# Rounding float64 weights on the chip: products on GpSimd, ScalarE's results in PSUM, two units' scores made earlier

## The chip, the cores and the metric

The kernel runs on one core of a Trainium2 chip. The metric is the device time of one execution in microseconds (us); the median of nine executions of the kernel before is 1681.1 us.

## The reference

Eight batches of eight heads attend over 576 tokens with 64 channels per head. Of each row of scores only the 32 largest are kept. The result, as 4608 tokens of 512 channels, goes through two matrix products with a leaky ReLU between them.

```python
scores = scale * np.matmul(q, k.transpose(0, 1, 3, 2))      # (8, 8, 576, 576)
kth = np.partition(scores, -32, axis=-1)[..., -32:-31]
scores = np.where(scores >= kth, scores, -1000000000.0)
attn = softmax(scores)                                       # with 1e-9 added to the sum
x = (attn @ v).transpose(0, 2, 1, 3).reshape(4608, 512)
h = x @ w_in                                                 # (4608, 2048)
out = np.maximum(0.01 * h, h) @ w_out                        # (4608, 512)
```

`w_in` (512 x 2048) and `w_out` (2048 x 512) arrive as float64. The host passes their bits as pairs of 32-bit words, and the kernel makes float32 of them itself.

## The kernel before, in words

**Units.** Attention is cut into 144 units. A unit is 128 rows of scores for both heads of a pair. It passes through these steps, on the engines named: `scores` (TensorE into the PSUM tiles `psc0` and `psc1`, then two ScalarE copies into `s_sb`), `top_k` on VectorE (eight MAX8 and six MATCH_REPLACE8 over 576 columns, lines 195 and 198), `mask` on GpSimd (for each head a TENSOR_SCALAR, line 209, and a TENSOR_TENSOR, line 211), `exponents` and `normalize` on ScalarE, transposes on TensorE with ScalarE copies, `weigh_values` on TensorE, and a ScalarE copy into `x` (line 272).

**Steps.** The instruction order on each engine is written out by hand. The loop over `s` takes in each step one unit through `top_k`, the one before through `mask`, the one before that through `exponents`, and so on, and it issues `scores` for the unit two steps ahead. After each 256 tokens (128 for the first two chunks) the two products of that chunk, `mlp`, become available. They are issued in portions between the other work: `ph` (line 282, `x` times `w_in`), a leaky ReLU on ScalarE into `gT` (line 288), then `pz` (line 294, `gT` times `w_out`).

**The gap.** After the first four units come six steps without a new unit (`gap`). In them the weights are converted, in 16 chunks of 128 x 1024 values: eight of `w_in`, then eight of `w_out`. Slots 1 to 3 of each gap step call `convert`, so there are 18 calls. The products of the first chunk of 128 tokens are also issued in the gap, and so are the scores of the fifth and the sixth unit (units 4 and 5, counted from 0), after slot 0 of the last two gap steps. These are the first units whose `top_k` follows the gap.

**One chunk.** A chunk's raw words lie in one of three `raw` buffers, `lo` and `hi` interleaved. On VectorE, line 110 takes the exponent field out of `hi`, line 111 the upper mantissa bits (written straight into the weight tile `dst`). Every other chunk (`on_vector`) is clamped by line 114 on VectorE and shifted by line 115 on ScalarE; the others are clamped and shifted by three ScalarE instructions, lines 117 to 119. ScalarE's line 120 turns the low word into `frac`, in place in `raw`. Two calls later three VectorE instructions finish the chunk: line 122 adds the two parts of the mantissa, line 124 puts the sign into the power of two, line 126 multiplies. Lines 122, 124 and 126 each read two tiles of SBUF. Line 124 is the last reader of the raw buffer; the fetch of the chunk three later waits for it on SyncE's queue, which issues all DMAs.

Of the kernel before, what the change touches and what calls it, by code (L numbers as in the profile page):

```python
# [8 lines left out]
F32 = mybir.dt.float32  # L9
U32 = mybir.dt.uint32  # L10
AF = mybir.ActivationFunctionType
ALU = mybir.AluOpType
# [5 lines left out]
def kernel(  # L18
# [13 lines left out]
    nc = tc.nc  # L32
    NPAIR, P, S = qT.shape
# [12 lines left out]
    WCH = 1024  # L46
# [7 lines left out]
    const = ctx.enter_context(tc.tile_pool(name="const", bufs=1))  # L54
    xpool = ctx.enter_context(tc.tile_pool(name="xpool", bufs=2))
    loads = ctx.enter_context(tc.tile_pool(name="loads", bufs=LOADED))
    raws = ctx.enter_context(tc.tile_pool(name="raws", bufs=3))
    work = ctx.enter_context(tc.tile_pool(name="work", bufs=2))
    small = ctx.enter_context(tc.tile_pool(name="small", bufs=5))
    ps_sc = ctx.enter_context(tc.tile_pool(name="ps_sc", bufs=1, space=bass.MemoryType.PSUM))  # L60
# [3 lines left out]
    ident = const.tile([P, P], F32, name="ident")  # L64
    make_identity(nc, ident)

    ends = const.tile([P, 2], F32, name="ends")
    range_lo, range_hi = ends[:, 0:1], ends[:, 1:2]
    nc.vector.memset(range_lo, -896.0)
    nc.vector.memset(range_hi, 255.0)  # L70

    w_in = [const.tile([P, DFF], F32, name=f"w_in{c}") for c in range(HP)]
    w_out = [const.tile([P, 4, DMODEL], F32, name=f"w_out{c}") for c in range(NFC // 4)]
    gT = [const.tile([P, CHMAX], F32, name=f"gT{f}") for f in range(NFC)]
# [3 lines left out]
    def weight_chunks():  # L78

        words = moe_w_in.shape[1] // DFF  # L80
        for j in range(DFF // WCH):
            for c in range(HP):
                yield (w_in[c][:, j * WCH:(j + 1) * WCH],
                       moe_w_in[c * P:(c + 1) * P, j * WCH * words:(j + 1) * WCH * words])
        for f in range(0, NFC, 2):
            yield (w_out[f // 4][:, f % 4:f % 4 + 2, :],
                   moe_w_out[f * P:(f + 2) * P, :].rearrange("(g p) n -> p g n", g=2))
# [11 lines left out]
        nc.sync.dma_start(to, src)  # L99
        return dst, raw  # L100

    def convert_weights(dst, raw, on_vector):

        lo, hi = raw[:, :, 0], raw[:, :, 1]
        frac, man = lo.bitcast(F32), dst.bitcast(U32)
        ex = raws.tile([P, WCH], U32, name="ex", bufs=2)
        exf = ex.bitcast(F32)
        nc.vector.tensor_scalar(ex, hi, 20, 0x7FF, ALU.logical_shift_right, ALU.bitwise_and)  # L110
        nc.vector.tensor_scalar(man, hi, 0xFFFFF, None, ALU.bitwise_and)  # L111

        if on_vector:
            nc.vector.tensor_scalar(ex, ex, 1151.0, 896.0, ALU.min, ALU.max)  # L114
            nc.scalar.activation(ex, ex, AF.Copy, bias=-896.0 * 2.0 ** 23, scale=2.0 ** 23)
        else:
            nc.scalar.activation(exf, ex, AF.Relu, bias=range_lo, scale=1.0)
            nc.scalar.activation(exf, exf, AF.Relu, bias=range_hi, scale=-1.0)
            nc.scalar.activation(ex, exf, AF.Copy, bias=255.0 * 2.0 ** 23, scale=-2.0 ** 23)
        nc.scalar.activation(frac, lo, AF.Copy, bias=1.0, scale=2.0 ** -52)  # L120
        yield
        nc.vector.scalar_tensor_tensor(out=dst, in0=man, scalar=2.0 ** -20, in1=frac,  # L122
                                       op0=ALU.mult, op1=ALU.add)
        nc.vector.scalar_tensor_tensor(out=ex, in0=hi, scalar=0x80000000, in1=ex,  # L124
                                       op0=ALU.bitwise_and, op1=ALU.bitwise_or)
        nc.vector.tensor_tensor(dst, dst, exf, ALU.mult)  # L126

# [2 lines left out]
    def load_qk(pi):  # L132
        qt = loads.tile([P, S], F32, name="qt")
        kt = loads.tile([P, S], F32, name="kt")
        nc.sync.dma_start(qt, qT[pi])
        nc.sync.dma_start(kt, kT[pi])
        qk_of[pi] = qt, kt

    def load_v(pi):
        v_of[pi] = loads.tile([P, NKC, 2, D], F32, name="vt", bufs=LOADED_V)  # L140
        nc.sync.dma_start(v_of[pi], vk[pi])
# [19 lines left out]
    units = []  # L161
# [8 lines left out]
    def scores(u):  # L170
        ps = [ps_sc.tile([P, 2, 512], F32, name=f"psc{i}") for i in range(2)]
        for n in range(0, len(u.parts), 2):
            for half in range(2):
                for i, pi, side, r0 in u.parts[n:n + 2]:
                    qt, kt = qk_of[pi]
                    d = slice(side * D, (side + 1) * D)
                    nc.tensor.matmul(  # L177
                        ps[i][r0:r0 + u.rows, half, 0:HS],
                        qt[d, u.q0:u.q0 + u.rows],
                        kt[d, half * HS:(half + 1) * HS],  # L180
                        start=True, stop=True,
                    )
        u.both = work.tile([P, 2, S], F32, name="s_sb", bufs=5)
        u.s = [u.both[:, i, :] for i in range(2)]
        for i in range(2):
            nc.scalar.copy(u.s[i].rearrange("p (h n) -> p h n", h=2), ps[i][:, :, 0:HS])  # L186
# [26 lines left out]
    def exponents(u, i):  # L213
        nc.scalar.activation(u.s[i], u.s[i], AF.Exp, bias=u.nbias[:, i:i + 1], scale=SCALE,  # L214
                             accum_out=u.z[:, i:i + 1])

    def sums(u):
        u.ze = small.tile([P, 2], F32, name="ze")
        nc.scalar.activation(u.ze, u.z, AF.Copy, bias=1e-9, scale=1.0)  # L219
# [109 lines left out]
    LAG = 3  # L329


    FIRST, GAP = 4, 6
    steps = units[:FIRST] + [None] * GAP + units[FIRST:]
    gap = range(FIRST, FIRST + GAP)

    def unit(n):
        return steps[n] if 0 <= n < len(steps) else None
# [17 lines left out]
    def slot_budget(s):  # L355

        after = [at for at, _ in ready_at if at >= s]
        until = gap[-1] if s in gap else after[0] if after else s
        return backlog[0] / ((until + 1 - s) * SLOTS)

    SLOTS = 7
    converting, begun = [], [0]

    chunks, raw_chunks = weight_chunks(), []

    def fetch_weights():
        chunk = next(chunks, None)
        got = load_weights(*chunk) if chunk else None
        if got:
            raw_chunks.append(got)  # L370

    def convert():

        if len(converting) == 2 or not raw_chunks:
            for c in converting[:1]:
                next(converting.pop(0), None)
        if raw_chunks:
            begun[0] += 1
            converting.append(convert_weights(*raw_chunks.pop(0), on_vector=begun[0] % 2 == 1))
            next(converting[-1])  # L380
        fetch_weights()

    with tc.manual_schedule():
        last = {p: n for n, u in enumerate(steps) if u for p in u.pairs}
        for p in range(HP):
            load_qk(p)
            if p < 2:
                scores(units[p])
        for _ in range(3):
            fetch_weights()  # L390
        for p in range(HP):
            load_v(p)

        def load_more(s):

            for of, load, n, lag in ((qk_of, load_qk, LOADED, -2), (v_of, load_v, LOADED_V, LAG)):
                while len(of) < NPAIR and (len(of) < n or last[len(of) - n] + lag <= s):
                    load(len(of))

        for s in range(len(steps) + LAG):  # L400
            cur, old = unit(s), unit(s - 1)
            older, oldest, new = unit(s - 2), unit(s - LAG), unit(s + 2)
            picks = top_k(cur) if cur else iter(())
            budget = slot_budget(s)

            def slot(n):
                next(picks, None)
                if s in gap and n:
                    convert()

            slot(0)
            if new and s in gap:
                scores(new)
            if old:
                mask(old, 0)
                mask(old, 1)
            mlp_steps(budget)
            if older:
                exponents(older, 0)
            if oldest:  # L420
                transpose_main(oldest, 0)
            mlp_steps(budget)
            if older:
                exponents(older, 1)
                sums(older)
            slot(1)
            if oldest:
                transpose_main(oldest, 1)
            mlp_steps(budget)
            if oldest:  # L430
                transpose_tail(oldest)
            slot(2)
            mlp_steps(budget)
            if older:
                reciprocals(older)
            mlp_steps(budget)
            slot(3)
            if older:
                normalize(older, 0)
                normalize(older, 1)  # L440
            if oldest:
                weigh_values(oldest)
            if new and s not in gap:
                scores(new)
            mlp_steps(budget)
            mlp_steps(budget)
            attended(s)
            if s >= gap[-1]:
                load_more(s)
        mlp_steps(1e9)  # L450
# [53 lines left out]
```

## Time and profile before

| | |
|---|---|
| median of 9 runs (lowest, highest) | 1681.1 us (1680.71, 1682.39) |
| the profiled execution: its own time | 1682.27 us |
| the profiled execution: span from first to last instruction | 1680.6 us |
| mean granted TensorE clock | 0.981 |
| TensorE busy | 1555.4 us (93%) |
| VectorE busy | 1493.5 us (89%) |
| ScalarE busy | 1005.8 us (60%) |
| GpSimd busy | 1081.3 us (64%) |
| the gap on VectorE: first line 110 to first MAX8 of unit 4 | 46.18 to 138.92 us |

In the profile PE is TensorE's matmuls, PEld its weight loads, DVE is VectorE, ACT is ScalarE, POOL is GpSimd and SP is SyncE. Shares are averages over stages of different kinds: four units alone, the gap, a stretch in which VectorE is busy all the time and TensorE is not, and then a long stretch in which TensorE is. What the gap costs is read in the gap. A VectorE instruction's record begins up to 0.08 us before the one ahead has ended, so costs in a full queue are read from start to start.

### The profile page before, as it was taken

To read this page: it belongs to the slowest core of one execution; us is meant where nothing else is said; L and a number is where in the kernel's file an instruction comes from. 1 tells how busy PE (TensorE), PEld (TensorE's weight loads), DVE (VectorE), ACT (ScalarE), POOL (GpSimd) and SP (SyncE) were. 2 spreads that over 40 slices of the span, in tenths; PEclk is the share of its full clock that TensorE was granted. 3 is DMA by queue.
4 is the path that set the end of the run, shared out by engine and by line. 5 is a ranking of instruction groups with operands and counts; after the bars stand their busy time and mean duration, and the time that the engine had idled before them with its cause. 6 is when DMAs were issued, how large, how long until landed. Compare 5 with 4: busy or idle time off the path is not lost.

```text
span 1680.6 us, 25687 instructions
## 1 busy us (share of the span) xinstructions
PE 1555.4 (93%) x9360; PEld 1057.0 (63%) x9360; DVE 1493.5 (89%) x3114; ACT 1005.8 (60%) x2277; POOL 1081.3 (64%) x726
## 2 busy tenths in 40 slices
PE   3365679999999999999999999999999999999999
PEld 2252465757576757676767676767676767676765
DVE  8999999999999999999999999999999999999700
ACT  2762566666666666666656565656565656565630
POOL 5203777777777777777777777777777777777700
PEclk9977799999999999999999999999999999999999
DMA  4451001000200011000110011000100010000000
GB/s 162 136 189 43 1 29 49 19 14 15 63 26 13 1 43 43 30 1 29 49 37 1 13 33 54 17 13 20 59 24 13 1 41 16 22 1 13 1 13 13
DMA packets 22462, 57.21 MB, mean 34 GB/s; under 512 B 2368, under 2 KB 2368, under 8 KB 21312
## 3 DMA queue, kind: packets, MB, share of 16 engines
q1 hardware_dynamic: 22336, 55.58, 9.7%
q8 instruction: 73, 1.20, 0.3%
q14 instruction: 53, 0.43, 0.1%
HBM read 46.14 MB, written 9.44 MB: 33 GB/s over the span
## 4 chain that ended last, share of the span: by engine, by line
PE 84%; DVE 14%; ACT 1%; issue 0%; DMA 0%; SPq 0%; ACTq 0%
PE ph L282 29%; PE pz L294 29%; PE po L262 10%; PE psc L177 9%; PE main L234 7%; DVE tops L195 6%; DVE rest L198 5%; PE tail L240 1%; DVE ex L124 1%; DVE w_in L126 1%; DVE w_in L122 1%; DVE ex L110 0%; DVE w_in L111 0%; ACT raw L120 0%; DVE ex L114 0%
## 5 line engine op out<-in xcount | busy, mean ns | idle before, releaser
L209 POOL TENSOR_SCALAR pen<-s_sb,tops 128x576 f32<-128x576 f32 x288 | 639.3, 2220 | 385.4 <-PE ph L282 157.7
L195 DVE MAX8 tops<-rest 128x8 f32<-128x576 f32 x864 | 607.9, 745 | 0.0
L282 PE MATMUL ph<-x,w_in 128*128 128x256 f32 (+1 forms) x2432 | 560.3, 376 | 19.5 <-ACT gT L288 14.2
L294 PE MATMUL pz<-w_out,gT 128*128 128x512 f32 x1152 | 534.8, 599 | 1.4 <-ACT gT L288 1.4
L282 PEld LDWEIGHTS ph<-x,w_in 128*128 128x128 f32 x2432 | 431.3, 194 | 104.7 <-ACT x L272 29.5
L198 DVE MATCH_REPLACE8 rest<-tops,rest 128x576 f32<-128x576 f32 x576 | 423.3, 743 | 0.0
L211 POOL TENSOR_TENSOR s_sb<-s_sb,pen 128x576 f32<-128x576 f32 x288 | 407.8, 1416 | 24.0
L294 PEld LDWEIGHTS pz<-w_out,gT 128*128 128x128 f32 x1152 | 203.3, 190 | 218.4 <-issue 215.4
L226 ACT ACTIVATE s_sb<-s_sb,rz 128x576 f32<-128x576 f32 x288 | 206.9, 768 | 75.2 <-DVE rz L223 75.1
L186 ACT COPY s_sb<-psc 128x576 f32<-128x576 f32 x288 | 169.9, 642 | 104.3 <-PE psc L177 104.3
L214 ACT ACTIVATE s_sb<-s_sb,nbias 128x576 f32<-128x576 f32 x288 | 223.5, 776 | 14.7 <-POOL s_sb L211 14.7
L235 ACT COPY wT<-main 128x512 f32<-128x512 f32 x288 | 166.2, 578 | 107.7 <-PE main L234 107.6
L288 ACT ACTIVATE gT<-ph 128x256 f32<-128x256 f32 (+1 forms) x304 | 113.1, 374 | 192.4 <-PE ph L282 192.4
L234 PE MATMUL main<-ident,s_sb 128*128 128x128 f32 x1152 | 167.0, 279 | 64.9 <-ACT s_sb L226 64.4
L262 PEld LDWEIGHTS po<-wT,vt 128*64 128x64 f32 x3200 | 164.2, 141 | 93.2 <-ACT s_sb L226 47.8
L234 PEld LDWEIGHTS main<-ident,s_sb 128*128 128x128 f32 x1152 | 141.7, 144 | 120.1 <-issue 55.9
L262 PE MATMUL po<-wT,vt 128*64 128x128 f32 (+1 forms) x3200 | 198.6, 274 | 18.5 <-ACT wT L235 18.5
L198 DVE MATCH_REPLACE8 rest<-tops,s_sb 128x576 f32<-128x576 f32 x288 | 211.6, 742 | 0.0
L195 DVE MAX8 tops<-s_sb 128x8 f32<-128x576 f32 x288 | 202.0, 743 | 6.6 <-ACT s_sb L186 6.6
L177 PE MATMUL psc<-kt,qt 64*128 64x288 f32 (+1 forms) x1280 | 189.4, 441 | 6.7 <-DMA kt<-in_kT_dram 4.5
L177 PEld LDWEIGHTS psc<-kt,qt 64*128 64x128 f32 (+1 forms) x1280 | 103.5, 182 | 50.9 <-issue 22.8
L223 DVE RECIPROCAL rz<-ze 128x2 f32<-128x2 f32 x144 | 23.6, 164 | 98.3 <-ACT ze L219 98.3
(33 smaller groups left out, 490.5 us busy)
## 6 DMA issues: line engine op xcount, KB each, us to landing
vt<-in_vk_dram SPq DMA_DIRECT2D x32, 320.0 KB, 3.1
qt<-in_qT_dram SPq DMA_DIRECT2D x32, 288.0 KB, 3.0
kt<-in_kT_dram SPq DMA_DIRECT2D x32, 288.0 KB, 3.3
out_dram<-o_sb SPq DMA_DIRECT2D x36, 256.0 KB, 2.0
raw<-in_moe_w_in_dram SPq DMA_DIRECT2D x8, 1024.0 KB, 5.3
raw<-in_moe_w_out_dram SPq DMA_DIRECT2D x8, 1024.0 KB, 4.8
```

Of the source, the lines that this page charges most:

```text
L177: nc.tensor.matmul(ps[i][r0:r0 + u.rows, half, 0:HS], qt[d, u.q0:u.q0 + u.rows], kt[d, half * HS:(half + 1) * HS], start=True, stop=True,)
L186: nc.scalar.copy(u.s[i].rearrange("p (h n) -> p h n", h=2), ps[i][:, :, 0:HS])
L195: nc.vector.max(out=u.tops[:, i, r, :], in_=src[i])
L198: nc.vector.match_replace(out=rest[i], in_to_replace=u.tops[:, i, r, :], in_values=src[i], imm_value=LOWEST)
L209: nc.gpsimd.tensor_scalar(pen, u.s[i], u.tops[:, i, ROUNDS - 1, 7:8], MASKED, ALU.is_lt, ALU.mult)
L211: nc.gpsimd.tensor_tensor(u.s[i], u.s[i], pen, ALU.add)
L214: nc.scalar.activation(u.s[i], u.s[i], AF.Exp, bias=u.nbias[:, i:i + 1], scale=SCALE, accum_out=u.z[:, i:i + 1])
L226: nc.scalar.activation(u.s[i], u.s[i], AF.Copy, bias=0.0, scale=u.rz[:, i:i + 1])
L234: nc.tensor.transpose(main[:, c, :], u.s[i][:, k0:k0 + P], ident)
L262: nc.tensor.matmul(po[side * D:(side + 1) * D, o, :], vt[:, c, side, :], u.wT[:, c + side * (NKC - 1) if c + 1 < NKC else 2 * (NKC - 1), r ...
L282: nc.tensor.matmul(ph[:, 0:n], w_in[c][:, f * P:(f + 1) * P], x[c][:, 0:n], start=(c == 0), stop=(c == HP - 1),)
L294: nc.tensor.matmul(pz[0:m, 0:DMODEL], gT[f][:, r0:r0 + m], w_out[f // 4][:, f % 4, :], start=(f == 0), stop=(f == NFC - 1),)
```

## The change

All 16 chunks are now clamped on VectorE (line 114 of before becomes line 107 and is no longer in every other chunk only), and ScalarE does two instructions for each. Their results, `frac` and `power`, go into the PSUM tiles `psc0` and `psc1`, which `scores` uses outside the gap, so the two VectorE instructions that read them now read one tile of SBUF and one of PSUM each. The final product moves from VectorE (line 126) to GpSimd (line 119). `ex` gets three buffers instead of two. The constants `ends` go.

A call of `convert` now begins a chunk (three VectorE instructions), finishes the chunk of the call before (two VectorE instructions, one GpSimd), and then issues the ScalarE part of the new one. A chunk is finished one call after it was begun, not two.

Units 4 and 5 get their scores at the ends of steps 2 and 3, before the gap, and none are issued in the gap.

```diff
-    def convert_weights(dst, raw, on_vector):
+    def convert_weights(dst, raw):
         lo, hi = raw[:, :, 0], raw[:, :, 1]
-        frac, man = lo.bitcast(F32), dst.bitcast(U32)
-        ex = raws.tile([P, WCH], U32, name="ex", bufs=2)
-        exf = ex.bitcast(F32)
+        man = dst.bitcast(U32)
+        ex = raws.tile([P, WCH], U32, name="ex")
         nc.vector.tensor_scalar(ex, hi, 20, 0x7FF, ALU.logical_shift_right, ALU.bitwise_and)
         nc.vector.tensor_scalar(man, hi, 0xFFFFF, None, ALU.bitwise_and)
-        if on_vector:
-            nc.vector.tensor_scalar(ex, ex, 1151.0, 896.0, ALU.min, ALU.max)
-            nc.scalar.activation(ex, ex, AF.Copy, bias=-896.0 * 2.0 ** 23, scale=2.0 ** 23)
-        else:
-            nc.scalar.activation(exf, ex, AF.Relu, bias=range_lo, scale=1.0)
-            nc.scalar.activation(exf, exf, AF.Relu, bias=range_hi, scale=-1.0)
-            nc.scalar.activation(ex, exf, AF.Copy, bias=255.0 * 2.0 ** 23, scale=-2.0 ** 23)
+        nc.vector.tensor_scalar(ex, ex, 1151.0, 896.0, ALU.min, ALU.max)
+        yield
+        frac, power = (ps_sc.tile([P, 2, 512], F32, name=f"psc{i}").rearrange("p h n -> p (h n)")
+                       for i in range(2))
+        power = power.bitcast(U32)
         nc.scalar.activation(frac, lo, AF.Copy, bias=1.0, scale=2.0 ** -52)
+        nc.scalar.activation(power, ex, AF.Copy, bias=-896.0 * 2.0 ** 23, scale=2.0 ** 23)
         yield
         nc.vector.scalar_tensor_tensor(out=dst, in0=man, scalar=2.0 ** -20, in1=frac, ...)
-        nc.vector.scalar_tensor_tensor(out=ex, in0=hi, scalar=0x80000000, in1=ex, ...)
+        nc.vector.scalar_tensor_tensor(out=ex, in0=hi, scalar=0x80000000, in1=power, ...)
-        nc.vector.tensor_tensor(dst, dst, exf, ALU.mult)
+        nc.gpsimd.tensor_tensor(dst, dst, ex.bitcast(F32), ALU.mult)
...
     def convert():
-        if len(converting) == 2 or not raw_chunks:
-            for c in converting[:1]:
-                next(converting.pop(0), None)
-        if raw_chunks:
-            begun[0] += 1
-            converting.append(convert_weights(*raw_chunks.pop(0), on_vector=begun[0] % 2 == 1))
-            next(converting[-1])
+        chunk = convert_weights(*raw_chunks.pop(0)) if raw_chunks else iter(())
+        next(chunk, None)
+        while converting:
+            next(converting.pop(0), None)
+        next(chunk, None)
+        converting.append(chunk)
         fetch_weights()
...
-            older, oldest, new = unit(s - 2), unit(s - LAG), unit(s + 2)
+            older, oldest, new = unit(s - 2), unit(s - LAG), None
+            if s not in gap:
+                new = units[s + 2] if s < FIRST else unit(s + 2)
...
-            if new and s in gap:
-                scores(new)
...
-            if new and s not in gap:
+            if new:
                 scores(new)
```

More of the change, by code (lines that the diff above doesn't have):

```diff
@@ L65 @@
     make_identity(nc, ident)
[L67 to L70, printed above, removed]
     w_in = [const.tile([P, DFF], F32, name=f"w_in{c}") for c in range(HP)]
@@ L123, in convert_weights @@
                                        op0=ALU.mult, op1=ALU.add)
-        nc.vector.scalar_tensor_tensor(out=ex, in0=hi, scalar=0x80000000, in1=ex,
+        nc.vector.scalar_tensor_tensor(out=ex, in0=hi, scalar=0x80000000, in1=power,
                                        op0=ALU.bitwise_and, op1=ALU.bitwise_or)
-        nc.vector.tensor_tensor(dst, dst, exf, ALU.mult)
+        nc.gpsimd.tensor_tensor(dst, dst, ex.bitcast(F32), ALU.mult)
     qk_of, v_of = {}, {}
@@ L361 @@
     SLOTS = 7
-    converting, begun = [], [0]
+    converting = []
     chunks, raw_chunks = weight_chunks(), []
```

## The prediction

> **What bounds the kernel now.** I read the page's slices first, then its chain, to learn which engine sets the time where.
>
> ```profile
> PE   3365679999999999999999999999999999999999
> DVE  8999999999999999999999999999999999999700
> PE 84%; DVE 14%; ACT 1%; issue 0%; DMA 0%; SPq 0%; ACTq 0%
> ```
>
> Each slice is 42 us. VectorE is full from the start, TensorE only from the seventh slice on. The chain in order of time (start, us, what) shows where the one hands over to the other, and what it runs through in the gap:
>
> ```profile
> 107.23 1.03 ACT raw L120
> 108.47 1.22 PE ph L282 x4
> 109.69 2.22 PE psc L177 x8
> ...
> 137.78 1.23 DVE w_out L126
> 139.01 1.32 DVE tops L195 x2
> ...
> 281.57 1.46 DVE rest L198 x2
> ...
> 287.92 2.59 PE ph L282 x12
> ```
>
> The gap lies wholly on the chain: up to 103 us and after 135 us by VectorE, between by ScalarE and TensorE. From 139 to 283 us VectorE's top-k sets the pace, then TensorE to the end. Neither of these later stretches is touched, so what the gap's end (138.92 us) moves, the end moves. Everything below is therefore the new time of that one point.
>
> The list of waits in 46 to 140 us (us in total, times, longest) says what held VectorE:
>
> ```profile
> ACT s_sb L186 <- PE psc L177: 6.8, 2, 3.4
> DVE w_out L122 <- ACT raw L120: 6.6, 2, 3.8
> ```
>
> VectorE waited 6.6 us for ScalarE, which had itself stood twice for the scores of units 4 and 5. The rest of the gap VectorE was busy, and the question is what a chunk costs it. The timeline of VectorE (start, us, instruction), first where GpSimd still masks unit 3, then alone:
>
> ```profile
> 47.60 1.14 DVE L114 TENSOR_SCALAR ex<-ex 128x1024 uint32<-128x1024 uint32 x1
> 48.67 1.89 DVE L110 TENSOR_SCALAR ex<-raw 128x1024 uint32<-128x1024 uint32 x1
> 50.48 0.68 DVE L111 TENSOR_SCALAR w_in<-raw 128x1024 uint32<-128x1024 uint32 x1
> ...
> 53.93 2.32 DVE L126 TENSOR_TENSOR w_in<-w_in,ex 128x1024 f32<-128x1024 f32 x1
> ...
> 61.74 0.69 DVE L110 TENSOR_SCALAR ex<-raw 128x1024 uint32<-128x1024 uint32 x1
> ...
> 65.34 1.23 DVE L126 TENSOR_TENSOR w_in<-w_in,ex 128x1024 f32<-128x1024 f32 x1
> ```
>
> and of GpSimd in the same stretch:
>
> ```profile
> 48.28 1.72 POOL L211 TENSOR_TENSOR s_sb<-s_sb,pen 128x576 f32<-128x576 f32 x1
> 50.10 3.05 POOL L209 TENSOR_SCALAR pen<-s_sb,tops 128x576 f32<-128x576 f32 x1
> 53.23 1.93 POOL L211 TENSOR_TENSOR s_sb<-s_sb,pen 128x576 f32<-128x576 f32 x1
> ```
>
> This is the heart of the matter. The same L110 takes 0.69 us alone and 1.89 us beside a GpSimd TENSOR_TENSOR; L126 takes 1.23 and 2.32. In both cases VectorE's instruction ends one solo duration (less 0.1 us) after GpSimd's has ended: it stood still while GpSimd ran. And GpSimd got in between two VectorE instructions standing back to back (L114, L110). The change puts a GpSimd TENSOR_TENSOR into every chunk. The groups on the page price it:
>
> ```profile
> L211 POOL TENSOR_TENSOR s_sb<-s_sb,pen 128x576 f32<-128x576 f32 x288 | 407.8, 1416 | 24.0
> ```
>
> The group of L207 (two columns) has a mean of 233 ns; so a column costs (1416 - 233) / 574 = 2.06 ns, and 1024 columns 233 + 1022 x 2.06 = 2340 ns.
>
> **The change part by part.**
>
> *VectorE's own work for a chunk.* From start to start in the quiet part: L110 0.61, L111 0.60, L114 0.60, L122 1.14, L124 1.14 us. Where the next instruction waits for another engine, as L110 does behind L126, it starts 0.03 us after the end instead of 0.08 before: 0.11 more. Sum 4.20 us. Before, a chunk took 5.46 (with L114) or 4.86 us, mean 5.16. So 16 products at 1.25 go and 8 clamps at 0.60 come. L122 and L124 now read one operand from PSUM, and no row shows VectorE doing that. The nearest rows are ScalarE's: 642 ns for 576 columns out of PSUM (L186), 768 ns out of SBUF (L226), so PSUM need not be dearer; L124's own spread of 1211 to 1225 ns says little. I bound it at 0.07 us either way per instruction (0.13 a chunk, about 2 us in all) and take zero. [...]
>
> *The product on GpSimd.* Chunk n's product is released by the end of its second scalar_tensor_tensor. At that moment VectorE's queue goes straight on to the three bit operations of chunk n+2. The first of these starts ahead of GpSimd, which has a semaphore to wait for; GpSimd's request falls into it and, if it is served as at 48.7 us, gets in ahead of the second. That one then waits. How long? L110 lost 1.89 - 0.69 = 1.20 us to a product of 576 columns; times 1024/576 is 2.13 us. Ends: by L126's loss of 1.09 us, 1.94; by the whole product, 2.34; and nothing at all if GpSimd loses the race (first rival). I take 2.13, because the row is that of the very instruction. After it, the clamp and the two scalar_tensor_tensors run on; beside GpSimd's L209, L122 with two SBUF operands lost 0.38 us, but GpSimd is done by then. [...]
>
> *The period* is then 4.20 + 2.13 = 6.33 us.
>
> *The start of the gap* is in the old trace. The five bit operations of chunks 0 and 1 end up where they were, at 51.08 us. The second clamp comes next, 0.60 plus the 0.38 that L122 lost to L209 there: 52.06. Two scalar_tensor_tensors, 2.28: 54.34. Reciprocal and wait, 0.16: 54.5 us.
>
> *Sum.* From there 14 periods (chunks 2 to 15 begin, 1 to 14 finish): 14 x 6.33 = 88.6. Last, chunk 15's two instructions, 2.3, with no bit operation behind for GpSimd to block. 54.5 + 88.6 + 2.3 = 145.4 us against 138.9: 6.5 us later.
>
> *What I cost at nothing.* ScalarE has two instructions a chunk (1.06 and 1.14 us) where it had two or four. Its first now waits for PSUM that VectorE frees one chunk earlier; queued behind it are the leaky ReLUs for which TensorE waits. It has 6.33 - 1.14 = 5.2 us for 2.2 plus a pair of ReLUs, for which 16 matmul records took 2.05 us. Without that cover the old 6.6 us of waiting come back. The fetches on SyncE's queue now wait for the chunk finished one call earlier; one period lies between release and use, and landing took 4.7 to 5.3 us, once 6.2. That is hidden at 6.33, not at 4.20. GpSimd's queue holds unit 3's masks ahead of the products (done at 54.6, before the first is ready) and unit 4's behind them (9 us later). TensorE gets the last weights 2.4 us after VectorE is done, in front of the scores of unit 6, needed two units (19 us) later.
>
> *The moved scores* cost TensorE 2 x 2.8 us, the first while it idles from 16 to 36 us, the second behind unit 0's values, and ScalarE 2 x 1.2 us. ScalarE idles from 39.6 to 45.0; the second pair pushes the first `frac` to about 51.1 us, needed at 52.06. Nothing, then. They also take away the two stops of ScalarE; that is already in the sum, which has no such wait.
>
> **The numbers.** Against the profiled execution's own time, 1682.27 us (span 1680.6): 1688.8. It stands 1.2 above the median, so the median becomes 1681.1 + 6.5 = 1687.6 us. With the ends of the delay it is +3.9 to +9.5, and PSUM makes it +2 to +11.5.
>
> **The rivals.**
>
> *First: VectorE keeps its turn through all three bit operations* and GpSimd runs beside the two scalar_tensor_tensors, which no longer need two SBUF operands. Their 2.28 us nearly hold a product. For it: L209 at 50.10 took 3.05 us instead of 2.22, while L111 right after L110 lost nothing, so there GpSimd was passed over. Against it: both TENSOR_TENSORs got in at the next boundary. Then VectorE's 4.20 us are not the limit either: a fetch is released by one chunk and used one chunk later, so two periods must hold 4.20 + 5.2, a period of 4.70. 54.5 + 65.8 + 2.3 = 122.6: 16.3 us earlier, 1664.8 us. The point between the two: 14 periods fit the old gap at (138.9 - 54.5 - 2.3) / 14 = 5.86 us, a mean delay of 1.66 us per chunk.
>
> *Second: mixed turns.* GpSimd gets in at some chunks only, with a mean delay of 1.0 to 1.8 us: periods 5.2 to 6.0, -9 to +2 us, about 1677.
>
> *Third: the waiting of ScalarE returns on top of the delay.* In order behind leaky ReLUs that wait for products made later than before, `frac` comes late as at 117.6 and 135.4 us: 6.6 us more, +13, 1694. Against it: the two old stops came from the scores in the gap.
>
> **Chances.** Blocked at every chunk 0.50, VectorE keeping its turn 0.30, mixed 0.10, the third 0.10. About 0.2% (3.4 us) is what a measurement of this kernel tells from no change. Of the first case 0.05 falls within it; of the mixed case half is faster, half within. Faster 0.35, same 0.10, slower 0.55. The range takes in the first rival and nearly all of the third: 1663 to 1694; the likeliest case alone, 1683 to 1693.
>
> **What would show it.** In the new timeline one of the three bit operations in each chunk from the third on should take 2.6 to 2.9 us instead of 0.69, the product on GpSimd about 2.4 to 2.9 us, and the first MAX8 of unit 4 should start near 145 us. If all three stay at 0.7 us and VectorE idles for `raw`, the first rival holds. Idle time before the scalar_tensor_tensors, put down to ScalarE, is the third. If the first MAX8 moves and the end does not move with it, my reading of the chain is wrong.

## The result, and the profile after

The changed kernel takes 1687.37 us (median of 9 runs, 1687.17 to 1687.46); the kernel before 1681.19 us (29 runs). The ratio is 1.0035, with a 95% interval of 1.0027 to 1.0043: slower, by 6.2 us between the medians. The profiled executions differ by 5.2 us (1687.44 against 1682.27).

The chain of the changed kernel in order of time (start, us, what) hands over at the same places as before, only later:

```profile
46.28 0.82 DVE ex L105
...
54.58 0.65 DVE ex L105
55.23 2.75 DVE w_in L106
57.98 0.60 DVE ex L107
58.58 1.13 DVE w_in L115
...
144.21 1.32 DVE tops L188 x2
...
286.77 1.46 DVE rest L191 x2
...
293.12 2.59 PE ph L275 x12
```

The gap begins as before and ends 5.2 us later, and TensorE takes over 5.2 us later (293.12 against 287.92). Inside the gap it is the second bit operation, line 106, that is long. VectorE's timeline shows one chunk's period (start, us, instruction):

```profile
60.77 0.68 DVE L105 TENSOR_SCALAR ex<-raw 128x1024 uint32<-128x1024 uint32 x1
61.37 2.84 DVE L106 TENSOR_SCALAR w_in<-raw 128x1024 uint32<-128x1024 uint32 x1
64.14 0.68 DVE L107 TENSOR_SCALAR ex<-ex 128x1024 uint32<-128x1024 uint32 x1
64.74 1.21 DVE L115 SCALAR_TENSOR_TENSOR w_in<-w_in,psc 128x1024 f32<-128x1024 uint32 x1
65.87 1.20 DVE L117 SCALAR_TENSOR_TENSOR ex<-raw,psc 128x1024 uint32<-128x1024 uint32 x1
67.00 0.68 DVE L105 TENSOR_SCALAR ex<-raw 128x1024 uint32<-128x1024 uint32 x1
```

and GpSimd's timeline shows what stands beside it:

```profile
60.92 2.74 POOL L119 TENSOR_TENSOR w_in<-w_in,ex 128x1024 f32<-128x1024 f32 x1 [3.49 <-DVE ex L117]
67.15 2.73 POOL L119 TENSOR_TENSOR w_in<-w_in,ex 128x1024 f32<-128x1024 f32 x1 [3.49 <-DVE ex L117]
```

The product starts 0.15 us into line 105, waits until that is done (its record is 2.74 us, while unhindered it takes 2.37 to 2.38, as the third experiment shows), and then line 106 waits until the product is done. This happens in each of the 14 chunks that have a product beside them; line 106 is short (0.68 us) only in the first two. In the list of waits for the gap VectorE does not occur: it waits neither for `raw` nor for ScalarE.

### The profile page after: what moved, and what is told of

Same layout as the page of the kernel before. It is cut to its first block, busy times and chain, and to the rows that moved or that the text cites. A ratio compares the mean times of both kernels' runs of the same rounds, so it can differ in the third digit from the quotient of the medians.

```text
span 1685.7 us, 25684 instructions
## 1 busy us (share of the span) xinstructions
PE 1559.6 (93%) x9360; PEld 1059.3 (63%) x9360; DVE 1506.3 (89%) x3104; ACT 988.3 (59%) x2261; POOL 1123.7 (67%) x742
## 4 chain that ended last, share of the span: by engine, by line
PE 83%; DVE 16%; issue 1%; ACT 0%; DMA 0%; SPq 0%; ACTq 0%
PE ph L275 28%; PE pz L287 28%; PE po L255 10%; PE psc L170 9%; PE main L227 7%; DVE tops L188 6%; DVE rest L191 5%; DVE w_out L106 1%; DVE w_in L106 1%; PE tail L233 1%; DVE ex L105 1%; DVE ex L107 1%; DVE w_in L115 1%; DVE w_out L115 1%; DVE ex L117 0%
```

## The experiments

My theory (the lock theory of the expectations below): the product on GpSimd holds up one bit operation a chunk, that alone turned the change from a gain into a loss, and it would cost little elsewhere. The rivals: it is the new order of finishing a chunk, or PSUM, or a GpSimd product slows VectorE wherever it stands, or the delay is a fixed price of taking turns.

| run | median us | gap ends at us |
|---|---|---|
| before | 1681.19, 1681.66 and 1681.97, measured anew beside each set of runs | 138.92 |
| after | 1687.37 | 144.12 |
| e1: product on VectorE | 1677.42 | 133.76 |
| e2: before, scores ahead alone | 1677.64 | 133.40 |
| e3: product beside lines 115 and 117 | 1666.20 | 122.56 |
| e4: results in SBUF | 1690.61 | 146.34 |
| e5: e3 with results in SBUF | 1693.43 | 149.71 |
| e6: half a product | 1673.01 | 129.93 |
| e7: scores back in the gap | 1694.25 | 152.86 |
| e8: e3 with four raw buffers | 1661.76 | 117.78 |

In all ten the profiled execution's own time less the end of the gap lies between 1543.3 and 1543.7 us. What the gap's end moves, the end moves: that reading of the chain is shown. A little of what moves the gap's end is no edit's work: between these executions the first MAX8 of unit 0 starts anywhere from 7.32 us (e5) to 8.26 us (e4), and everything up to the gap with it.

**e1, the product back on VectorE.**

```diff
-        nc.gpsimd.tensor_tensor(dst, dst, ex.bitcast(F32), ALU.mult)
+        nc.vector.tensor_tensor(dst, dst, ex.bitcast(F32), ALU.mult)
```

> The changed kernel with one part undone: the final product is on VectorE again. Lock theory (GpSimd's product holds up the second bit operation of each chunk for 2.2 us, and that alone made the change slower): every bit operation takes 0.7 us again, a chunk costs VectorE what a chunk with the clamp cost before, 5.46 us, so the gap ends near 56.0 + 14 x 5.46 + 3.6 = 136 us instead of 144.1, and the time is about 8 us below the changed kernel's, 1679 us, which is 2 to 3 us below the kernel before. Rival (the new order of finishing a chunk one call earlier, or PSUM, is what costs): the product on VectorE adds 1.25 us to each of the 16 chunks, 20 us, and the time rises to about 1700 us or, if half of that hides, 1690 us or more.

Measured 1677.42 us, 0.9975 of the kernel before [0.9965, 0.9985]. From VectorE's timeline:

```profile
61.51 0.69 DVE L106 TENSOR_SCALAR w_in<-raw 128x1024 uint32<-128x1024 uint32 x1
...
65.09 1.23 DVE L119 TENSOR_TENSOR w_in<-w_in,ex 128x1024 f32<-128x1024 f32 x1
```

Line 106 is short again, and taking 16 products of 1.2 us off VectorE cost 10 us. The rest of the change is a gain of some 4 us, and the order of finishing is not what costs. The gap ended 2 us earlier than I had worked out, as a period is 5.33 us and not 5.46.

**e2, the kernel before with the scores ahead.** The last three pieces of the change's diff, alone.

```diff
-            older, oldest, new = unit(s - 2), unit(s - LAG), unit(s + 2)
+            older, oldest, new = unit(s - 2), unit(s - LAG), None
+            if s not in gap:
+                new = units[s + 2] if s < FIRST else unit(s + 2)
...
-            if new and s in gap:
-                scores(new)
...
-            if new and s not in gap:
+            if new:
```

> The kernel before with one part of the change done: the scores of units 4 and 5 are issued before the gap; conversion is as before. My reading of the chain (ScalarE's two stops for these scores are what VectorE waited 6.6 us for): the gap ends at 138.9 - 6.6 = 132.3 us and the time is about 6.6 us below the kernel before, 1674.6 us; the two waits for the scores are gone from the list. Rival (ScalarE is late there anyway, because it has four instructions for every second chunk and the leaky ReLUs between them): other waits take their place and the time falls by less than 3 us.

Measured 1677.64 us, 0.9973 [0.9962, 0.9984]; the gap ends 5.5 us earlier. That is less than the 6.6 us of my account and more than the rival's 3. The list of waits still has VectorE waiting for ScalarE:

```profile
DVE w_out L122 <- ACT raw L120: 0.9, 2, 0.5
DVE w_in L122 <- ACT raw L120: 0.7, 1, 0.7
```

6.6 us of waiting became 1.6: 0.7 behind the exponents and copies of a unit ahead of the gap, 0.9 behind leaky ReLUs and a four-instruction chunk. So this part is worth 4 us between medians (5.5 in the profiles), and e1, which has it too, shows that clamps, PSUM and order come to nothing measurable in sum; of the three, only PSUM is measured by itself below (e4).

**e3, the product released later.** A tiny GpSimd instruction ahead of each product but the last two reads two columns of the clamp's result of the chunk two later. The product is issued one call later. (Not shown: the lines that keep the `ex` tiles of all chunks begun in the list `exs`, and those that make `convert` issue the product one call later.)

```diff
+        yield
+        if len(exs) > mine + 1:
+            nc.gpsimd.tensor_scalar(gate, exs[-1].bitcast(F32)[:, 0:2], 1.0, None, ALU.mult)
         nc.gpsimd.tensor_tensor(dst, dst, ex.bitcast(F32), ALU.mult)
```

> The changed kernel, with each product on GpSimd held back by a tiny GpSimd instruction that reads two columns of the clamp's result of the chunk two later, so that the product starts behind that chunk's three bit operations and runs beside the two instructions that read one operand from PSUM. Lock theory: these do not need what GpSimd holds; a chunk costs VectorE 4.1 us and some 0.4 to 0.7 us of overhang or of waiting for the next fetch, period 4.6 to 4.9 us; the gap ends near 54.5 + 14 x 4.8 + 2.3 = 124 us and the time is about 20 us below the changed kernel's, 1667 us. Rival (a GpSimd product slows VectorE whatever runs beside it, by memory traffic or by any access): the period stays near 6.2 us and the time near 1687 us, with the delay now in the scalar_tensor_tensors.

Measured 1666.20 us, 0.9908 [0.9893, 0.9923]. VectorE's and GpSimd's timelines:

```profile
64.32 0.69 DVE L110 TENSOR_SCALAR ex<-raw 128x1024 uint32<-128x1024 uint32 x1 [0.49 <-POOL w_in L127]
64.93 0.69 DVE L111 TENSOR_SCALAR w_in<-raw 128x1024 uint32<-128x1024 uint32 x1
65.53 0.69 DVE L112 TENSOR_SCALAR ex<-ex 128x1024 uint32<-128x1024 uint32 x1
66.13 1.22 DVE L120 SCALAR_TENSOR_TENSOR w_in<-w_in,psc 128x1024 f32<-128x1024 uint32 x1
67.26 1.22 DVE L122 SCALAR_TENSOR_TENSOR ex<-raw,psc 128x1024 uint32<-128x1024 uint32 x1
```

```profile
66.38 0.21 POOL L126 TENSOR_SCALAR gate<-ex 128x2 f32<-128x2 f32 x1 [2.09 <-DVE ex L112]
66.56 2.38 POOL L127 TENSOR_TENSOR w_in<-w_in,ex 128x1024 f32<-128x1024 f32 x1
```

The same instructions, one tiny one more, and neither engine slows the other: the product takes 2.38 us beside two instructions that take their usual 1.22. That the product slows whatever runs beside it is refuted.

**e4, ScalarE's results in SBUF.**

```diff
-        frac, power = (ps_sc.tile([P, 2, 512], F32, name=f"psc{i}").rearrange("p h n -> p (h n)")
-                       for i in range(2))
-        power = power.bitcast(U32)
+        frac, power = lo.bitcast(F32), ex
```

> The changed kernel with one part undone: ScalarE's results go back into SBUF, in place in the raw words and in the exponent tile. Lock theory: in the changed kernel the product never runs beside the two scalar_tensor_tensors (it ends 0.8 us before the next of them starts), so where their operands lie makes no difference: 1687 us, within 2 us. [...]

Measured 1690.61 us, 1.0050 [1.0037, 1.0063]: 3.2 us above the changed kernel, more than I allowed. The gap ends 2.2 us later. VectorE's and GpSimd's timelines give 1.2 of it:

```profile
54.05 2.44 DVE L115 SCALAR_TENSOR_TENSOR ex<-raw,ex 128x1024 uint32<-128x1024 uint32 x1
```

```profile
54.00 1.41 POOL L202 TENSOR_TENSOR s_sb<-s_sb,pen 128x576 f32<-128x576 f32 x1
```

With two SBUF operands this instruction (line 117 of the changed kernel, where it took 1.21 us beside the same mask) waits for unit 3's mask, once. Another 0.8 us is a later begin of the gap (46.96 us). It is not the edit's: the first MAX8 of unit 0 is already 0.76 us late (8.26 against 7.50 us), as the first `scores` waited for the first `kt` fetch until 5.29 us instead of 4.54. The last 0.2 us is left of a wait for a fetch, below. The other 15 chunks' scalar_tensor_tensors take 1.21 to 1.23 us, as with PSUM (1.20 to 1.22). The profiled execution stands 1.0 us below the median, and what makes up that rest is open. So PSUM by itself cost and saved nothing per instruction here.

That wait for a fetch shows one thing more. Once VectorE stood idle for it when a product began:

```profile
113.93 1.78 DVE L105 TENSOR_SCALAR ex<-raw 128x1024 uint32<-128x1024 uint32 x1 [1.22 <-DMA raw<-in_moe_w_out_dram]
115.63 0.68 DVE L106 TENSOR_SCALAR w_out<-raw 128x1024 uint32<-128x1024 uint32 x1
```

```profile
112.79 2.37 POOL L117 TENSOR_TENSOR w_out<-w_out,ex 128x1024 f32<-128x1024 f32 x1 [3.50 <-DVE ex L115]
```

Here the product started first and runs unhindered, line 105 is held up (1.78 us) and line 106 is not (0.68). So it is not line 106 as such that waits, for its data or its buffer, but the bit operation that comes up while the product runs: line 105 here, line 106 in the changed kernel.

**e5, both: the product beside lines 115 and 117, with results in SBUF.** The edits of e3 and e4.

> As e3 (each product held back until it runs beside the two scalar_tensor_tensors), but ScalarE's results lie in SBUF again, so these two read two tiles of SBUF each. Lock theory: now the product holds them up for its whole length less the overlap at its start; a chunk costs VectorE about 6.2 us again and the time is back near 1687 us, 20 us above e3. So PSUM is worth nothing where the product stands beside the bit operations (e4) and everything where it stands beside the scalar_tensor_tensors. Rival (a scalar_tensor_tensor never competes with GpSimd; line 126 lost 1.09 us for being a TENSOR_TENSOR): 1666 us as e3.

Measured 1693.43 us, 1.0070 [1.0057, 1.0084]: 27 us above e3. From the two timelines, one chunk first and then the end of the gap on VectorE:

```profile
63.78 1.22 DVE L118 SCALAR_TENSOR_TENSOR w_in<-w_in,raw 128x1024 f32<-128x1024 uint32 x1
64.91 1.22 DVE L120 SCALAR_TENSOR_TENSOR ex<-raw,ex 128x1024 uint32<-128x1024 uint32 x1
68.39 0.69 DVE L110 TENSOR_SCALAR ex<-raw 128x1024 uint32<-128x1024 uint32 x1 [2.26 <-POOL w_in L125]
...
143.12 3.37 DVE L118 SCALAR_TENSOR_TENSOR w_out<-w_out,raw 128x1024 f32<-128x1024 uint32 x1
146.42 3.37 DVE L120 SCALAR_TENSOR_TENSOR ex<-raw,ex 128x1024 uint32<-128x1024 uint32 x1
```

```profile
64.03 1.05 POOL L124 TENSOR_SCALAR gate<-ex 128x2 f32<-128x2 f32 x1 [2.10 <-DVE ex L112]
65.05 3.31 POOL L125 TENSOR_TENSOR w_in<-w_in,ex 128x1024 f32<-128x1024 f32 x1
```

Here VectorE's instructions started first, and GpSimd is the one that waits: 1.05 us for two columns, 3.31 for the product (0.21 and 2.38 in e3). VectorE pays afterwards, when its next chunk needs the `ex` buffer that the product still reads. I had expected the wait on the other engine, and 20 us of it instead of 27. Of the 7 us more, 1.2 are unit 3's mask again, as in e4 (line 120 takes 2.45 us at 53.12), and 4.3 come at the end of the gap: no bit operations stand between the last two chunks, and lines 118 and 120 take 3.37 us each instead of 1.22, which I read as the engines waiting for each other in turn. ScalarE, which writes `ex` in place here, comes behind the tiny instruction that reads it (41.4 us of waiting), but VectorE never waits for ScalarE in the list of this run. PSUM is what makes e3 possible (27 us); in the changed kernel it had nothing to do, except once (1.2 us).

**e6, half a product.**

```diff
-        nc.gpsimd.tensor_tensor(dst, dst, ex.bitcast(F32), ALU.mult)
+        half = slice(0, WCH // 2)
+        nc.gpsimd.tensor_tensor(dst[:, half], dst[:, half], ex.bitcast(F32)[:, half], ALU.mult)
```

> The changed kernel with the product of only the first 512 of each chunk's 1024 columns (the other half of the weights is left without its power of two). Lock theory: the second bit operation waits as long as the product runs, so its delay of 2.15 us falls to about 1.1 us, the period to 5.15 us; 14 x 1.07 = 15 us less, 1672 us. Rival (the delay is a fixed price of changing turns between the engines): the bit operation still takes 2.8 us and the time stays at 1687 us.

Measured 1673.01 us, 0.9949 [0.9936, 0.9963]. VectorE's timeline:

```profile
60.74 1.76 DVE L106 TENSOR_SCALAR w_in<-raw 128x1024 uint32<-128x1024 uint32 x1
```

The bit operation itself is unchanged, and its delay fell with the product's length, from 2.15 to 1.08 us. It is the product's duration that is paid, not a fixed price.

**e7, the scores back in the gap** of the changed kernel.

```diff
-            older, oldest, new = unit(s - 2), unit(s - LAG), None
-            if s not in gap:
-                new = units[s + 2] if s < FIRST else unit(s + 2)
+            older, oldest, new = unit(s - 2), unit(s - LAG), unit(s + 2)
...
+            if new and s in gap:
+                scores(new)
...
-            if new:
+            if new and s not in gap:
```

> The changed kernel with one part undone: the scores of units 4 and 5 are issued in the last two gap steps again. My account (with a period of 6.2 us ScalarE has room for these two stops, and psc0 and psc1 are only lent): ScalarE has to wait twice for TensorE, 3.4 us each as before, in front of a chunk's first instruction; it had 3.7 us of waiting for VectorE there, so nothing or up to 4 us: 1687 to 1691 us. Rival (the scores ahead are worth their full 4 us, e2, here too, or more, since the scores now stand in line for the PSUM tiles of the conversion): 1691 to 1697 us.

Measured 1694.25 us, 1.0077 [1.0064, 1.0089]: 6.9 us above the changed kernel, as the rival said. The timelines of TensorE, ScalarE and VectorE:

```profile
122.38 3.42 PE L170 MATMUL psc<-kt,qt 64*128 64x288 f32 x8 [2.55 <-DVE w_out L115]
```

```profile
124.89 0.64 ACT L179 COPY s_sb<-psc 128x576 f32<-128x576 f32 x1 [6.23 <-PE psc L170]
```

```profile
131.70 1.22 DVE L115 SCALAR_TENSOR_TENSOR w_out<-w_out,psc 128x1024 f32<-128x1024 uint32 x1 [4.28 <-ACT psc L112]
```

TensorE has to wait for VectorE to give the PSUM tiles back, ScalarE waits 6.2 us instead of 3.4 for TensorE, and VectorE then 4.3 us for ScalarE. My expectation left out the first of these waits. At 150 us VectorE waits 4.1 us again and ScalarE 6.3; there TensorE is busy with `pz` until 145.42 us, and VectorE has freed the first tile at 145.37.

**e8, what limits e3 taken away.** In e3 VectorE still waited now for the product (0.5 us, above), now for a fetch (1.1 us at most).

The edit against e3; in `exs` there are now the `dst` tiles.

```diff
-    LOADED, LOADED_V = 6, 5
+    LOADED, LOADED_V = 5, 4
-        raw = raws.tile([P, WCH, 2], U32, name="raw")
+        raw = raws.tile([P, WCH, 2], U32, name="raw", bufs=4)
...
-            nc.gpsimd.tensor_scalar(gate, exs[-1].bitcast(F32)[:, 0:2], 1.0, None, ALU.mult)
+            nc.gpsimd.tensor_scalar(gate, exs[-1][:, 0:2], 1.0, None, ALU.mult)
...
-        for _ in range(3):
+        for _ in range(4):
             fetch_weights()
```

> As e3, with what limits e3 taken away: four raw buffers instead of three (q, k buffers five instead of six, v buffers four instead of five, to make room), and the tiny GpSimd instruction reads what the second bit operation has written, so that the product starts 0.6 us earlier. If e3's period of 4.7 us is made of VectorE's 4.1 and waits for the fetch and for GpSimd's product, these go: period 4.1 to 4.3, the gap ends near 54.4 + 14 x 4.2 + 2.3 = 115.5 us instead of 122.6, and the time falls by 7 us to 1659 us. Rival (another engine sets 4.7 us, ScalarE with its leaky ReLUs or TensorE with the first chunk's products, or the fewer q, k, v buffers cost later): 1664 us or more.

Measured 1661.76 us, 0.9882 [0.9867, 0.9897]: 20 us below the kernel before and the best version of all. It is 4.4 us below e3, where I had expected 7: the period is 4.35 us, not 4.2. VectorE's and GpSimd's timelines:

```profile
63.34 0.69 DVE L110 TENSOR_SCALAR ex<-raw 128x1024 uint32<-128x1024 uint32 x1 [0.19 <-POOL w_in L127]
```

```profile
60.46 0.52 POOL L126 TENSOR_SCALAR gate<-w_in 128x2 f32<-128x2 f32 x1 [1.50 <-DVE w_in L111]
60.94 2.37 POOL L127 TENSOR_TENSOR w_in<-w_in,ex 128x1024 f32<-128x1024 f32 x1
```

The tiny instruction now falls into the clamp (line 112) and waits for it (0.52 instead of 0.21 us); the product ends 0.2 us too late for the next chunk's `ex`. The fetch no longer appears among VectorE's waits.

## Why the prediction was right, point by point

The direction and the mechanism were right, and the three signs named for them came: line 106 takes 2.83 to 2.85 us in the 14 chunks, the product 2.73 to 2.79, and the first MAX8 of unit 4 starts at 144.12. The time lies 0.2 us from the forecast. That nearness owes 1.0 us to chance. The sum said that the gap ends 6.5 us later, and it ends 5.2 later; but the profiled execution of before stands 1.1 us above its median, and that of after 0.1 above its own, so that the medians differ by 6.2. What sets the executions of the kernel before apart (1680.4 to 1683.2 us) is open.

- *The start of the gap.* Worked out as 54.5 us from the old trace; line 105 of chunk 2 starts at 54.50.
- *The delay.* Taken as 2.13 us, by scaling what L110 lost. Line 106 takes 2.75 us from start to start instead of 0.60, so 2.15. The bound by L126's loss (1.94) was too low, that by the whole product (2.34) too high.
- *VectorE's own work.* This is the term that was off: 4.20 us against 0.60 + 0.60 + 0.60 + 1.13 + 1.13 = 4.06. I had added 0.11 for an instruction that waits for other engines, and line 105 follows line 117 with the usual overlap (0.07 us); VectorE had nothing to wait for there. The period is (135.51 - 54.50) / 13 = 6.23 us instead of 6.33, and 14 x 0.10 = 1.4 us is the 1.3 by which the gap's end was missed.
- *PSUM.* Zero was right: the two instructions take 1207 to 1209 ns in the mean in the changed kernel; with two SBUF operands before, lines 122 (`w_out`) and 124 took 1222 and 1218 ns. No run shows the 0.07 us per instruction that the range allows for PSUM, 2 us at either end: the difference is 0.009 to 0.015 us, and in e4, the changed kernel with two SBUF operands, the same two instructions take 1.21 to 1.23 us.
- *Who goes first.* The first rival needed VectorE to keep its turn through three bit operations. In all 14 chunks GpSimd was served after the first. What I held for that rival, L209's 3.05 us, is there again in the changed kernel (3.05 us at 50.12), and is not explained by any run; it has one SBUF tensor as its input, and the product two. In the 14 chunks line 105 (0.67 to 0.73 us) runs on while the product waits (2.73 to 2.79), then the product while line 106 waits (2.83 to 2.85). In 14 chunks of e5 the scalar_tensor_tensors with two SBUF operands run on (1.21 to 1.22 us) while the product waits (3.30 to 3.31). In e3 those with one operand in PSUM (1.21 to 1.22 us) and the product (2.37 to 2.38) leave each other alone. With line 202 (209 before), a GpSimd instruction too, not every bit operation waited: line 106 at 50.50 us took its usual 0.68 in the middle of those 3.05 us, and line 107 behind it 1.15. And the +9.5 us of the forecast's upper end, with the whole product as the delay, did not come.
- *What I cost at nothing.* ScalarE waits 40.6 us for VectorE in front of its line 112, so the cover held; the third rival did not come. The fetches were hidden at 6.23 us, and in e3, at 4.7 us, they were not, as said (VectorE waits 2.3 us for them, in three chunks).
- *The moved scores.* Nothing in the steps before the gap, as said: line 105 starts at 46.20 against 46.18 us. What they save was counted as the old 6.6 us; without the other parts it is 5.5 us of the gap (e2), in the changed kernel 8.4 (the two waits of e7). Between medians it is 4.0 and 6.9.

So the change is a gain of 4 us (scores ahead, e2) and a loss of 10 (the product on GpSimd, against e1); the rest comes to nothing in sum. What a part is worth depends on what else is there: in the changed kernel the scores ahead are worth 6.9.

## What to carry to other kernels

Before work goes from VectorE to GpSimd, ask which VectorE instructions will stand beside it at that moment, not how busy GpSimd is: 2.37 us of GpSimd work cost VectorE 2.15 us beside a bit operation that takes 0.69 alone (e1), and nothing beside the scalar_tensor_tensors with one operand in PSUM (1.21 to 1.22 us in e3, as in e1, where no product runs on GpSimd). Where a product is released by the end of the very instruction ahead of the sensitive ones, a tiny instruction that makes it wait for the last of these moves it to where it is free; here that was worth 21 us (e3 against the changed kernel). And read a shift at the place where the chain is handed over: ten kernels differed by 35 us there and by 0.4 us behind it.

## What the runs showed of the hardware that I had not expected

The waiting goes both ways, and even an instruction of two columns has to wait: GpSimd's takes 0.21 us where nothing holds it up (e3), 0.52 beside a bit operation (e8) and 1.05 beside a scalar_tensor_tensor with two SBUF operands (e5). And a VectorE instruction of 1024 columns with one operand in PSUM was no slower than with both in SBUF (1.21 us in the changed kernel, 1.21 to 1.23 in e4).
